# Constants of accumulating DMAs in SBUF instead of DRAM, 26 exponential slots instead of 30, output weights loaded later, two more packs on VectorE

## The chip, the cores and the metric

The kernel runs on one core of a Trainium2 chip. The metric is the device time of one execution in microseconds, as the median of several runs. The profile is one execution of its own, and its span reaches from its first to its last instruction.

## The reference

```
x = A_x                                    # 2048 tokens, 512 features; also the input of branch B
g = sigmoid((x * gate_w).sum(-1))          # one gate for each token
a = softmax(q k^T * 16 ** -0.5) v @ A_wo   # 32 heads of 16, over all 2048 keys; q, k, v from A_wqkv
b = (phi(q) (phi(k)^T v)) / (phi(q) z) @ B_wo   # linear attention, 32 heads of 16
    # phi(q) = [softmax(q w_phi), softmax(-q w_phi)], z = sum over tokens of phi(k)
return g * a + (1 - g) * b
```

Everything is in bf16. The softmax attention of branch A is by far the larger part: 32 x 2048 x 2048 scores.

## The kernel before

The softmax part is cut into 512 packs. A pack is one key tile of 128 tokens, four heads and 512 queries: four score tiles ("units") of 128 x 512. 16 packs in a row (the 16 key tiles) make a group, and 32 groups (4 query chunks x 8 sets of four heads) make the whole. TensorE computes the scores (L1025, `_scores`). They become weights in one of two ways:

- On ScalarE: one activation (L1073, `_exp`) takes two units from PSUM and writes exp(score) into two slots of the ring `ET`, which has `NSLOT` slots of 512. The value product of a pack (`_pv`, L1158) reads four slots and adds to the group's PSUM bank. A slot is free again once the pack that used it has been multiplied, so the exponential of the unit at place x waits for the value product of the unit at place x - NSLOT. TensorE may compute scores two activations ahead: scores k wait for exponential k - 2.
- On VectorE, for the packs that the bits of `AWAY` select in each group (131 of 512): a tensor_scalar from PSUM (L963, `_vector_bits`) writes the bits of a bf16 power of two into `va`, as uint16. Then the sum of four value products with shifted bits approximates the exponential (`_pv_terms`, L1158): `va` itself; two copies `vp` that VectorE makes by adding 62 and 95 to the bits (L980, `_vector_terms`, two packs at a time where there are two), one value side scaled; and `va` once more after 30 (`FIRST_SHIFT`) was added to it in place. This last addition is made by an accumulating DMA from POOL's queue (L1140), 512 KB, that reads a tensor `step` full of the constant 30. Only for the packs from 496 on does VectorE do it (L1146). `va` has room for three pairs of packs.

`step` is a tensor in DRAM: POOL fills a row of `va` with 30 (L593), and SP's queue stores it (L594). The first accumulating DMAs wait for this store.

Branch B (projections, softmax features by `_b_quad`, products, transposing DMAs) and the projections of branch A (L675, L748) run between the attention's instructions on the same engines. ScalarE has 16 long activations of branch B (L1331) among its exponentials. The gate's products stand in L772, and its exponential, L786, is on ScalarE. The output matmuls (L1461 with `WoB`, L1507 with `WoA`) come per query chunk, the first ones after more than half of the groups.

The order of the instructions on every engine is not written down but planned when the program is built (`Plan.order`): a list scheduler with a cost for each operation, a due pack (`prio`), an earliest pack (`rel`), a delay after the end (`lat`), and shifts of single due times by name in the table `SHIFT` ("p37" is the value product of pack 37, "b33" the bits of pack 33, "x33" its late value products, "i33" its first one and its DMA). At run time every engine follows its list in order and waits on semaphores. Accumulating DMAs are planned with a landing time of 6.2 us (`LANDING`), 3.2 us apart (`PACE`), and each waits for the landing of the second to last before it. SP's queue issues all other DMAs: x, weights, the splitting of q into padded tiles (L711), the turning of the normalised attention (L1198, L1413), the transposes of branch B and the output.

Of the kernel before, what the change touches and what calls it, by code (L numbers as in the profile page):

```python
# [404 lines left out]
class _Kernel:  # L405
    RING = 4
    NSLOT = 30
# [42 lines left out]
    def _memory(self, ctx):  # L450
# [55 lines left out]
        self.step = nc.dram_tensor("step", [P, self.NB * QCH], U16, kind="Internal").ap()  # L506
# [23 lines left out]
    def _loads(self):  # L530
# [24 lines left out]
        for j in range(1, self.NQC):  # L555
# [9 lines left out]
                 writes=[self.b_WoA], prio=-1, lat=4.0)  # L565
        self.dma("SP", "wob", lambda e: e.dma_start(self.WoB[:], self.B_wo.rearrange("(q p) j -> p q j", p=P)),
                 writes=[self.b_WoB], prio=-1, lat=4.0)

    def _consts(self):
# [22 lines left out]
        row = self.va[:, self.NVA - 1, 1].rearrange("p n q -> p (n q)")  # L592
        o = op("POOL", lambda e: e.memset(row, FIRST_SHIFT), 2.0, prio=-60)  # L593
        self.o_step = self.dma("SP", "step", lambda e: e.dma_start(self.step, row), cost=0.6, deps=[o], prio=-43, lat=6.0)  # L594
# [164 lines left out]
    def _gate(self):  # L759
# [44 lines left out]
    AWAY = (21, 22, 19, 29, 22, 27, 28, 29, 27, 31, 29, 23, 31, 22, 31, 31, 15, 31, 30, 29, 27, 29, 31, 14, 23, 31, 29, 31, 29, 23, 31, 31)  # L804

    SHIFT = (
# [761 lines left out]
```

## Time and profile before

| | |
|---|---|
| Time, median of 3 runs | 760.13 us (753.11 to 762.33) |
| Profiled execution, its own time | 753.26 us |
| Its span | 751.5 us |
| Granted TensorE clock | 0.997 |
| PE busy | 728.1 us (97%) |
| DVE busy | 700.2 us (93%) |
| ACT busy | 731.8 us (97%) |
| POOL busy | 126.5 us (17%) |
| Moved by DMA | 88.34 MB, of which 66.07 MB in queue q0 (accumulating DMAs) |
| HBM | 70.27 MB read, 2.62 MB written |

PE is TensorE's matmul, PEld its weight load, DVE is VectorE, ACT is ScalarE, POOL is GpSimd and SP is SyncE. A group of the profile's page reads: line, engine, operation, written tile <- read tile, count, then busy time, mean duration of one in ns, and the idle time of the engine just before the group with what ended most of it. Matmuls that use only a part of the array overlap, and so do successive activations, so that the sum of durations can be more than the time that passes. The chain is followed back from the last instruction: at each step to what released it, or to the instruction before it on its engine.

### The profile page before, as it was taken

How to read it: one execution, taken by the hardware profiler on the slowest of the kernel's cores; microseconds unless marked ns; L12 is line 12 of the kernel's file. 1: busy time of each engine (PE TensorE's matmuls, PEld its weight loads, DVE VectorE, ACT ScalarE, POOL GpSimd, SP SyncE). 2: the span in 40 equal slices, each digit the busy share in tenths (PEclk: the TensorE clock that was granted, in tenths of full speed). 3: DMA queues.
4: the chain of work that ended last, by engine and by line, in shares of the span. 5: the costliest groups of instructions: out<-in, count | busy, mean ns of one | idle time of the engine just before them, and what ended most of it. 6: DMA issues, size and time to landing. Idle time of an engine off the chain costs nothing.

```text
span 751.5 us, 16620 instructions
## 1 busy us (share of the span) xinstructions
PE 728.1 (97%) x6969; PEld 225.6 (30%) x6969; DVE 700.2 (93%) x1119; ACT 731.8 (97%) x782; POOL 126.5 (17%) x144
## 2 busy tenths in 40 slices
PE   8999999999999999999999999999999999999998
PEld 3233333333322232232222223233222232222222
DVE  6789999789999999999999999998999989999896
ACT  5899999999999999999999999999999999999996
POOL 4201011201101112021112210121121111121200
PEclk9999999999999999999999999999999999999999
DMA  9754246634655739485597973979496886786950
GB/s 225 200 89 82 31 84 113 104 60 63 118 96 82 144 57 161 85 139 89 96 159 140 177 123 54 181 132 158 70 168 120 140 145 114 143 154 111 170 98 29
DMA packets 108315, 88.34 MB, mean 118 GB/s; under 512 B 84944, under 2 KB 91472, under 8 KB 108240
## 3 DMA queue, kind: packets, MB, share of 16 engines
q0 software_dynamic: 18144, 66.07, 50.8%
q1 hardware_dynamic: 88368, 20.69, 15.2%
q8 instruction: 54, 0.88, 0.5%
q10 hardware_dynamic: 1728, 0.52, 0.3%
q14 instruction: 21, 0.17, 0.1%
HBM read 70.27 MB, written 2.62 MB: 97 GB/s over the span
## 4 chain that ended last, share of the span: by engine, by line
ACT 87%; PE 8%; DMA 4%; DVE 1%; POOL 0%; issue 0%; DVEq 0%; POOLq 0%
ACT ET L1073 83%; ACT bq L1331 4%; PE ps L1025 3%; PE ps L1158 3%; DMA WT<-nb 2%; DMA va<-step 1%; PE ps L675 1%; DMA xT<-in_A_x_dram 1%; PE ps L1461 1%; PE ps L748 0%; PE ps L1507 0%; DVE qT L731 0%; DVE bq L1302 0%; POOL bq L608 0%; ACT xT L1517 0%; DVE nb L1443 0%
## 5 line engine op out<-in xcount | busy, mean ns | idle before, releaser
L1073 ACT ACTIVATE ET<-ps 128x1024 bf16<-128x1024 f32 x762 | 703.9, 1141 | 10.0 <-PE ps L1025 9.7
L1025 PE MATMUL ps<-qT,kT 32*128 32x512 bf16 x2048 | 340.8, 385 | 11.1 <-ACT ET L1073 6.5
L963 DVE TENSOR_SCALAR va<-ps 128x512 uint16<-128x512 f32 x524 | 333.6, 680 | 16.5 <-PE ps L1025 15.3
L1140 POOL DMA_DIRECT2D va<-step x126 | 117.0, 988 | 583.1 <-DVE vp L980 246.5
L1025 PEld LDWEIGHTS ps<-qT,kT 32*128 32x128 bf16 x2048 | 90.1, 91 | 287.6 <-ACT ET L1073 227.3
L980 DVE TENSOR_SCALAR vp<-va 128x4096 uint16<-128x4096 uint16 (+1 forms) x148 | 159.9, 1094 | 5.8 <-PE ps L1158 5.2
L1158 PE MATMUL ps<-ET,V 128*32 128x512 bf16 x1524 | 145.6, 386 | 0.3 <-DVE bq L1302 0.2
L1158 PE MATMUL ps<-va,V 128*32 128x512 bf16 x1048 | 99.1, 386 | 2.4 <-DMA va<-step 2.0
L1158 PE MATMUL ps<-vp,vc 128*32 128x512 bf16 x1048 | 92.3, 387 | 2.6 <-DVE vp L980 2.5
L675 PE MATMUL ps<-WB,xT 128*128 128x512 bf16 x192 | 57.5, 384 | 0.0
L1158 PEld LDWEIGHTS ps<-ET,V 128*32 128x32 bf16 x1524 | 37.7, 94 | 64.5 <-issue 56.9
L1158 PEld LDWEIGHTS ps<-va,V 128*32 128x32 bf16 x1048 | 25.8, 95 | 39.0 <-issue 28.7
L675 PE MATMUL ps<-xT,WA 128*128 128x512 bf16 (+1 forms) x128 | 37.2, 381 | 0.1
L1158 PEld LDWEIGHTS ps<-vp,vc 128*32 128x32 bf16 x1048 | 23.5, 95 | 36.0 <-issue 21.4
L1331 ACT ACTIVATE bq<-bq 128x2048 bf16<-128x2048 bf16 x16 | 32.0, 2009 | 0.0
L1302 DVE CAST bq<-ps 128x512 bf16<-128x512 f32 x32 | 21.8, 682 | 3.8 <-PE ps L675 3.5
L1179 DVE STREAM_TRANSPOSE T<-ps 128x512 f32<-128x512 f32 x32 | 22.7, 709 | 2.6 <-PE ps L1158 2.5
L748 PE MATMUL ps<-WA,xT 128*128 128x128 bf16 x256 | 22.9, 221 | 0.0
L1165 PE MATMUL ps<-kT,zero 128*32 128x512 bf16 x240 | 22.7, 385 | 0.0
L1461 PE MATMUL ps<-WoB,WT 128*128 128x512 bf16 x64 | 19.6, 384 | 0.4 <-issue 0.4
L1329 DVE TENSOR_TENSOR bq<-bq,btree 128x2048 bf16<-128x2048 bf16 x16 | 19.5, 1218 | 0.0
L1507 PE MATMUL ps<-WoA,onTA 128*128 128x512 bf16 x64 | 18.6, 382 | 0.0
(84 smaller groups left out, 302.0 us busy)
## 6 DMA issues: line engine op xcount, KB each, us to landing
va<-step POOLq DMA_DIRECT2D x126, 512.0 KB, 6.0
turned<-T SPq DMA_DIRECT2D x240, 8.0 KB, 3.1
qT<-qs SPq DMA_DIRECT2D x120, 16.0 KB, 3.3
WB<-in_B_wqkv_dram SPq DMA_DIRECT2D x1, 1536.0 KB, 9.4
out_dram<-WB SPq DMA_DIRECT2D x12, 128.0 KB, 4.0
WA<-in_A_wqkv_dram SPq DMA_DIRECT2D x3, 384.0 KB, 5.7
step<-va SPq DMA_DIRECT2D x1, 512.0 KB, 8.5
WoA<-in_A_wo_dram SPq DMA_DIRECT2D x1, 512.0 KB, 10.3
```

The source lines that it names most:

```text
L675: ins = e.matmul(self._bank(job)[:, 0:n], lhs(c), rhs(c), start=(c == 0), stop=(c == 3))
L748: ins = e.matmul(self._bank(job)[:, P * tt:P * tt + P], self.xT[:, c, QCH * j + TOK * tt:QCH * j + TOK * tt + TOK], self.WA[:, 2, c, P * c ...
L963: parts.append(op("DVE", lambda e, j=j, job=job: e.tensor_scalar(self.va[:, pair, side, j, :], self._bank(job), SCALE * LOG2E * 128.0, (12 ...
L980: self.plan.op("DVE", lambda e, k=k, shift=shift: e.tensor_scalar(flat(self.vp[:, k]), flat(self.va[:, pair]), float(shift), None, op0=ALU ...
L1025: return e.matmul(out, self.kT[32 * i:32 * i + 32, cp, kt * TOK:(kt + 1) * TOK], self.qT[32 * i:32 * i + 32, s, :], start=True, stop=True, ...
L1073: o = plan.op("ACT", lambda e: e.activation(self.ET[:, a % NS:a % NS + n, :], self.ps[:, self._ring(a):self._ring(a) + n, :], ACT.Exp, sca ...
L1140: add = self.dma("POOL", f"add{p}", lambda e: e.dma_start(va.rearrange("p n q -> p (n q)"), self.step, accum_op=ALU.add), cost=self.ADD, d ...
L1158: ins = e.matmul(self._bank(ot)[32 * i:32 * i + 32, :], V[:, v0:v0 + 32], tile(), start=(kt == 0), stop=(kt == self.NT - 1), tile_position ...
L1165: ins = e.matmul(self._bank(ot)[32 * i:32 * i + 32, :], self.zero[:], self.kT[:, 0, 0:QCH], start=False, stop=False, tile_position=(0, 32 ...
L1179: op("DVE", lambda e: e.transpose(T1[:, side].rearrange("p b s -> p (b s)"), src()), 0.635, deps=last, writes=[b_T1[side]], name="n_t1", p ...
L1331: op("ACT", lambda e, side=side: e.activation(sides[side], sides[side], ACT.Exp, scale=1.0 - 2 * side), self.c_act(2048) + 0.04, reads=[bu ...
L1461: return e.matmul(self._bank(job), self.onTB[:, pr, tt * TOK:tt * TOK + TOK], self.WoB[:, pr, :], start=(pr == 0), stop=False)
```

## The change

`step` becomes a tensor in SBUF: 4 KB for each of the 128 partitions, filled by POOL, with no store. `NSLOT` goes from 30 to 26, which is 4 x 1 KB for each partition less. The loads of `WoA` and `WoB` get an earliest pack of 50 and 80 and a due pack of 60 and 90. `AWAY` selects 133 packs instead of 131 (one more in groups 6, 8, 21, 23 and 28, one less in groups 4, 14 and 27; in other groups it is only other packs), and `SHIFT` is another table, so that the planned order differs on every engine.

```diff
-    NSLOT = 30
+    NSLOT = 26
...
-        self.step = nc.dram_tensor("step", [P, self.NB * QCH], U16, kind="Internal").ap()
+        self.step = sb("step", [P, self.NB * QCH], U16)
...
         self.dma("SP", "woa", lambda e: e.dma_start(self.WoA[:], self.A_wo.rearrange("(q p) j -> p q j", p=P)),
-                 writes=[self.b_WoA], prio=-1, lat=4.0)
+                 writes=[self.b_WoA], prio=60, rel=50, lat=8.0)
         self.dma("SP", "wob", lambda e: e.dma_start(self.WoB[:], self.B_wo.rearrange("(q p) j -> p q j", p=P)),
-                 writes=[self.b_WoB], prio=-1, lat=4.0)
+                 writes=[self.b_WoB], prio=90, rel=80, lat=8.0)
...
-        row = self.va[:, self.NVA - 1, 1].rearrange("p n q -> p (n q)")
-        o = op("POOL", lambda e: e.memset(row, FIRST_SHIFT), 2.0, prio=-60)
-        self.o_step = self.dma("SP", "step", lambda e: e.dma_start(self.step, row), cost=0.6, deps=[o], prio=-43, lat=6.0)
+        self.o_step = op("POOL", lambda e: e.memset(self.step[:], FIRST_SHIFT), 2.0, prio=-10)
...
-    AWAY = (21, 22, 19, 29, 22, 27, 28, 29, 27, 31, 29, 23, 31, 22, 31, 31, 15, 31, 30, 29, 27, 29, 31, 14, 23, 31, 29, 31, 29, 23, 31, 31)
+    AWAY = (22, 22, 19, 29, 18, 30, 30, 30, 31, 31, 15, 23, 31, 28, 27, 31, 15, 31, 27, 15, 29, 31, 31, 15, 29, 31, 15, 27, 31, 30, 31, 31)
     SHIFT = (
-        ("p30", 2), ("e0", 12), ("p47", -10), ("e3", 4), ("g5", -13.5), ("p251", -1), ("p253", -11.5), ("p274", -4),
...
+        ("p8", 1), ("p13", -5), ("x25", 3), ("p16", -2.5), ("g0", -0.5), ("i5", 13.5), ("p14", 1), ("p20", -6.5),
...
-        self.b_va[self.NVA - 1][1].readers = [self.o_step]
...
-            add = self.dma("POOL", f"add{p}", lambda e: e.dma_start(va.rearrange("p n q -> p (n q)"), self.step, accum_op=ALU.add),
+            add = self.dma("POOL", f"add{p}", lambda e: e.dma_start(va.rearrange("p n q -> p (n q)"), self.step[:], accum_op=ALU.add),
```

221 rows, old and new, of the table SHIFT are left out of this document.

## The prediction

> **What bounds the kernel now.** I first read the busy shares, the queues and the groups of the page, to find the engine without slack.
>
> ```profile
> PE 728.1 (97%) x6969; PEld 225.6 (30%) x6969; DVE 700.2 (93%) x1119; ACT 731.8 (97%) x782; POOL 126.5 (17%) x144
> ...
> q0 software_dynamic: 18144, 66.07, 50.8%
> ...
> ACT 87%; PE 8%; DMA 4%; DVE 1%; POOL 0%; issue 0%; DVEq 0%; POOLq 0%
> ...
> L1073 ACT ACTIVATE ET<-ps 128x1024 bf16<-128x1024 f32 x762 | 703.9, 1141 | 10.0 <-PE ps L1025 9.7
> ...
> L963 DVE TENSOR_SCALAR va<-ps 128x512 uint16<-128x512 f32 x524 | 333.6, 680 | 16.5 <-PE ps L1025 15.3
> L1140 POOL DMA_DIRECT2D va<-step x126 | 117.0, 988 | 583.1 <-DVE vp L980 246.5
> L980 DVE TENSOR_SCALAR vp<-va 128x4096 uint16<-128x4096 uint16 (+1 forms) x148 | 159.9, 1094 | 5.8 <-PE ps L1158 5.2
> ```
>
> ScalarE's exponentials set the time: 762 of them are on 83% of the chain, and ScalarE is idle for only 751.5 - 731.8 = 19.7 us. So a change can save little unless it takes exponentials away; it can lose more easily. ScalarE's waits and the chain in order of time say where the idle time is:
>
> ```profile
> ACT ET L1073 <- PE ps L1025: 9.7, 6, 5.5
> ACT xT L1517 <- PE ps L1507: 4.5, 1, 4.5
> ```
>
> ```profile
> 22.41 8.16 DMA va<-step
> 30.61 0.93 PE ps L1158 x8
> ...
> 34.08 54.22 ACT ET L1073 x59
> ```
>
> 5.5 of the 9.7 us is the start, before the first scores. The chain shows the next largest: the first accumulating transfers, issued at 22.41, take 8.16 us to land while WB, WoA and WoB (2.5 MB) are loading. TensorE stands at L1158 until 30.61, and ScalarE loses 1.96 + 0.92 = 2.9 us by 34.07, as its timeline says. The remaining 9.7 - 5.5 - 2.9 = 1.3 us are three small gaps. The x59 row also gives the price of an exponential in a full stretch: 54.22 / 59 = 0.92 us, less than the 1.14 us of one, since they overlap.
>
> **Part 1: two more packs on VectorE (131 to 133).** A pack is 4 score tiles of 512, two exponentials of 1024. So 4 exponentials go: 4 x 0.92 = 3.7 us off ScalarE. VectorE gets 8 more L963 (8 x 0.68 = 5.4 us) and, as more packs come in pairs, four more L980 of 4096 at 1.22 and four fewer of 2048 at 0.68 (+2.2 us): 7.6 us. Two more transfers are issued, 0.9 us each, on a POOL queue that is 17% busy. Whether VectorE hides its 7.6 us is seen from the stretches:
>
> ```profile
> 200.00:300.00 100.00, 97.92 (x952) 28.29 (x952) 98.60 (x151) 100.00 (x108) 18.23 (x19) 1.00 0.61 104
> 400.00:500.00 100.00, 97.44 (x929) 29.92 (x926) 96.76 (x157) 99.99 (x108) 19.08 (x20) 1.00 0.77 134
> 500.00:520.00 20.00, 19.62 (x212) 6.29 (x208) 18.73 (x33) 20.00 (x23) 5.68 (x6) 1.00 1.00 171
> 580.00:612.00 32.00, 31.06 (x328) 9.71 (x324) 29.54 (x53) 31.38 (x35) 6.40 (x8) 1.00 0.97 157
> ```
>
> Columns are busy time of PE, PEld, DVE, ACT and POOL, then the clock, the share of the DMA engines and GB/s. Per group of 16 packs the count moves by +1 in groups 6, 8, 21, 23 and 28 and by -1 in 4, 14 and 27. Groups 21 and 23 lie near 480 to 560 us, where VectorE is 94 to 97% busy: two packs bring 2 x 3.8 us there, against about 2.7 us of idle time and no relief but what the planner moves elsewhere. That costs between 0 (the work moves) and 5 us (nothing moves). I take 1.5, nearer to hidden, because a pack's tiles are made up to three pairs ahead.
>
> **Part 2: 26 slots instead of 30.** An exponential now waits for the value products of the units 26, not 30, places before it: 13 exponentials (12 us) of reach instead of 15 (13.8). Most exponentials keep a wide margin. But in the changed order on TensorE two have none. Exponential 71 now needs the product of pack 37 (with 30 slots it would be pack 36, which stands far earlier), and TensorE's queue there reads: scores 72, the 16 gate products of L772, pack 37. Scores 72 wait for exponential 70, so nothing of this can run early. Exponential 77 needs pack 40 (with 30 slots pack 39, which is earlier), behind: scores 78, three projection halves of L675, pack 40. The prices are rows of the trace: scores 0.33 (0.39 with the tail of the pipeline), the gate about 1.0, four value products 0.33, L675 1.02 for four, so 0.26 each:
>
> ```profile
> 10.68 1.02 PE ps L675 x4
> ```
>
> ```profile
> 24.88 1.05 PE L772 MATMUL ps<-xT,bq 128*32 128x512 bf16 x16
> ```
>
> With about 0.3 us for the two hand-overs (an estimate, from the 0.04 us between PE and ACT at 34.07 and the gaps of some 0.2 us on the other side), ScalarE stands 0.3 + 0.33 + 1.0 + 0.33 = 2.0 us, and 0.3 + 0.33 + 6 x 0.26 + 0.33 = 2.5 us. Queued behind it on ScalarE are the next exponentials and the gate's own; on them wait TensorE's next scores. None of the long activations of L1331 (1.79 us), which in the old order cover such places, stands near these two. Together +4.5 us, at least 3 (if hand-overs are free and pipelines overlap) and at most 7 (VectorE has 15 evictions and 2 short terms at 0.68, a long term at 1.22 and a value copy at 0.54, 13.3 us, in the 12 exponentials before exponential 71, which last 11.0 us).
>
> **Part 3: weights later, no write of the constants.** The store of the constants (512 KB) and WoA and WoB (1 MB) leave the first 20 us; POOL's fill of the constants (1.80 us) moves behind other fills, ahead of 10 idle us. On SP's queue the loads are moved past the gate's 16 copies and two query splits. In the changed order the first transfer of constants is issued at about 20 us (after the first products of its pack), the second at about 23, and they are used behind scores 22 and 23, at 28 to 30 us. With landing times of 6 to 7 us the 2.9 us gap shrinks to about 0.5: -2.4 (bounds 0 and -2.9). The moved loads now fall between transfers of L1140 at 75 to 120 us; each can hold one back by the 2 us that the early crowding cost (8.16 against 6.0), which the margins of 3 us between issue and use there cover. Uncovered it would be 2 us each; I add nothing.
>
> **Part 4: constants read from SBUF.** This has no row. The landing now:
>
> ```profile
> DMA to landing us min/median/max: 5.3/6.0/11.0
> ```
>
> Queue q0 holds the 16 engines for 50.8% of 751.5 us, 382 us for 126 transfers: 3.03 us each, at 512 KB. A transfer reads the constants, reads the destination and writes it. Lower bound: the pace of the mix at 20 to 30 us, 307 GB/s at full share, gives 1.7 us. Upper bound: today 1.0 of the 1.5 MB is on the SBUF side, 346 GB/s in 3.03 us; if that were that side's limit, 1.5 MB would take 4.55 us. I take 3.03, since the nearest row is the transfer itself: same rows of 4 KB, same engine, same sum. Faster landings gain next to nothing, as TensorE waits for va only 2.0 + 3.0 us in all and its order is fixed; slower ones are the second rival.
>
> **The sum**, against the profiled execution (753.26 us, span 751.5): -3.7 + 1.5 + 4.5 - 2.4 = -0.1, so 753.2. The four executions shown (753.26, 760.13, 753.11, 762.33) have a mean of 757.2, 3.9 above the profiled one; a median may fall in either group, so I add that: **757 us**, against the 760.13 us of before no difference that a measurement of this kernel tells (about 2%, 15 us). Its own range is 748 to 767.
>
> **Rivals.**
>
> *All gaps close.* If the two stops of part 2 don't show, the early gap and the three small ones vanish and VectorE hides everything: 753.3 - 3.7 - 2.9 - 1.3 = 745. For it: these gaps all hang on crowded DMA engines. Against: the order of TensorE makes the stops unavoidable. It lies at the 2% bound from the median of before.
>
> *Constants from SBUF make the transfers slower.* Place: the bursts of L1140, where transfers follow each other at the pace of the engines. 24 of them already wait 49.9 us for a landing, and the engines are 97 to 100% taken at 500 to 520 and 580 to 612. The trace has 15 transfers in 57 us (374 to 431) and bursts of 8 to 9 in 26 to 35 us at 493, 537, 578 and 690. Up to about 3.8 us each they nearly fit; at 4.55 they overrun by 11 + 10 + 6 + 7 + 6 us and some 5 earlier: +45, near 800 us. Half way, at 4.2, about +25: 780. For it: all three streams are then on one side. Against: the read of HBM goes away. The Trainium skill's page "DMA: Bandwidth & Descriptors", section "Where 436 GB/s comes from", speaks against the change: the 16 SBUF ports are the bottleneck, at 435 GB/s. By it a transfer would take an estimated 2.4 us if only its two reads count and 3.6 us if the write counts too, and the time by the sum would be 757 to about 760. No run so far shows it.
>
> *The slots cost more than two stops.* Where VectorE is late, further exponentials wait for their slot; about 8 more stops of 2.2 us would give 775. For it: VectorE's 98.6% at 200 to 300 us. Against: elsewhere the margins in the order are as wide as before.
>
> **Chances.** Forecast 0.55; gaps close 0.12; slower transfers 0.23 (770 to 800); more stops 0.10. Faster by over 2%: 0.12; within: 0.55; slower: 0.33. The range, 744 to 788, reaches down to closed gaps and up past the middle of the slower transfers.
>
> **What would show it.** Right: 758 exponentials at 0.92 us; ScalarE idle for about 2 us twice between 75 and 90 us with TensorE at L772 and L675 ahead of it; no long wait at 28 to 34 us; landing near 6 us and q0 near 51%. Wrong: landing over 7.5 us with q0 above 60%; ScalarE waiting for L1158 in many places; VectorE idle less than 1% from 480 to 560 us.

## The result, and the profile after

The changed kernel takes 779.14 us (median of 4 runs, 777.55 to 781.4), the kernel before beside it 761.23 us (4 runs, 753.11 to 763.21): a ratio of 1.0294, interval 1.024 to 1.0349. It is slower by some 3%, where no change was forecast; the time lies inside the range given, but only because that range reached up to a rival that did not happen: by luck. Ratios here and below compare the fast executions alone, with a 95% interval, so they can differ from the ratio of the two medians. The profiled execution took 777.55 us, its span is 775.8 us, 24.3 us more than before.

The page of the changed kernel, the lines that answer to those shown of before:

```profile
PE 731.5 (94%) x6940; PEld 224.7 (29%) x7008; DVE 707.3 (91%) x1127; ACT 729.8 (94%) x778; POOL 129.8 (17%) x146
...
q0 software_dynamic: 18432, 67.12, 45.5%
...
ACT 60%; PE 22%; DVE 11%; DMA 4%; SPq 2%; issue 1%; DVEq 0%
...
L1071 ACT ACTIVATE ET<-ps 128x1024 bf16<-128x1024 f32 x758 | 702.9, 1138 | 34.8 <-PE ps L1023 30.2
...
L962 DVE TENSOR_SCALAR va<-ps 128x512 uint16<-128x512 f32 x532 | 339.6, 680 | 23.0 <-PE ps L1023 21.4
L1138 POOL DMA_DIRECT2D va<-step x128 | 119.2, 1017 | 607.0 <-DVE vp L979 364.2
```

ScalarE is busy for 2.0 us less and the span is 24.3 us longer, so it now idles 46.0 us instead of 19.7. All of the loss is idle time of ScalarE. TensorE is behind most of it (30.2 us before exponentials), but TensorE itself is idle more too (94% instead of 97%): something holds it. SP's queue (SPq), no part of before's chain, has 2% of this one. ScalarE's waits (us in total, times, longest):

```profile
ACT ET L1071 <- PE ps L1023: 30.2, 24, 6.4
ACT xT L1515 <- PE ps L1505: 5.9, 1, 5.9
ACT ET L1071 <- PE ps L1156: 4.1, 2, 2.3
```

The busy times by stretch tell where (columns as in the prediction: PE, PEld, DVE, ACT, POOL, then clock, DMA share, GB/s). First before, then after:

```profile
0.00:75.00 75.00, 71.23 (x650) 27.45 (x650) 58.06 (x102) 64.17 (x70) 16.66 (x26) 0.98 0.68 149
440.00:500.00 60.00, 58.88 (x521) 18.26 (x513) 57.91 (x94) 59.99 (x65) 7.50 (x9) 1.00 0.72 124
500.00:530.00 30.00, 28.46 (x287) 8.95 (x283) 26.44 (x49) 29.12 (x32) 5.68 (x6) 1.00 0.81 135
600.00:645.00 45.00, 44.37 (x411) 13.35 (x409) 42.83 (x72) 44.38 (x49) 7.84 (x9) 1.00 0.75 124
```

```profile
0.00:75.00 75.00, 71.77 (x679) 28.17 (x687) 60.68 (x98) 66.83 (x72) 18.58 (x27) 1.00 0.59 130
75.00:100.00 25.00, 24.33 (x213) 7.74 (x214) 20.36 (x42) 21.01 (x23) 1.72 (x2) 1.00 0.40 72
400.00:440.00 40.00, 37.37 (x389) 11.20 (x388) 34.44 (x59) 37.42 (x42) 9.31 (x9) 0.96 0.86 141
440.00:500.00 60.00, 55.99 (x445) 15.19 (x448) 52.73 (x83) 53.64 (x57) 6.97 (x8) 0.89 0.59 115
500.00:530.00 30.00, 23.65 (x227) 7.35 (x225) 22.68 (x39) 23.45 (x27) 4.36 (x5) 0.89 0.61 110
600.00:645.00 45.00, 38.09 (x355) 10.43 (x356) 33.79 (x56) 35.66 (x39) 7.80 (x9) 0.85 0.75 126
```

ScalarE's idle time is the stretch less its ACT column. It changes by -2.7 up to 75 us, +4.0 at 75 to 100 (before had 25.00 of 25), +2.6, +6.4, +5.7 and +8.7 in the four stretches between 400 and 645, and +1.4 at the output. That makes 26.1 of the 26.3 us. The first two were forecast, the four in the middle (23.4 us) were not. ScalarE's timeline of the changed kernel (start, time, group, idle before):

```profile
76.46 1.94 ACT L1071 ACTIVATE ET<-ps 128x1024 bf16<-128x1024 f32 x2 [1.82 <-PE ps L1156]
...
84.45 9.27 ACT L1071 ACTIVATE ET<-ps 128x1024 bf16<-128x1024 f32 x10 [2.27 <-PE ps L1156]
...
473.52 1.02 ACT L1071 ACTIVATE ET<-ps 128x1024 bf16<-128x1024 f32 x1 [1.85 <-PE ps L1023]
...
525.95 1.02 ACT L1071 ACTIVATE ET<-ps 128x1024 bf16<-128x1024 f32 x1 [5.60 <-PE ps L1023]
...
632.70 1.02 ACT L1071 ACTIVATE ET<-ps 128x1024 bf16<-128x1024 f32 x1 [6.36 <-PE ps L1023]
634.21 1.02 ACT L1071 ACTIVATE ET<-ps 128x1024 bf16<-128x1024 f32 x1 [0.48 <-PE ps L1023]
635.72 1.02 ACT L1071 ACTIVATE ET<-ps 128x1024 bf16<-128x1024 f32 x1 [0.49 <-PE ps L1023]
```

With one at 428 (1.53) the four late stops are 15.3 us. The other 9.5 us of the 24.8 that ScalarE idles in the four stretches come behind them: after a stop exponentials follow each other at 1.51 us (632.70, 634.21, 635.72) and not at 0.92. The clock column says why. The stretch behind the stop at 473, in the view by stretch:

```profile
473.60:487.20 13.60, 13.13 (x70) 2.42 (x63) 8.48 (x14) 9.13 (x9) 0.68 (x1) 0.50 0.56 115
```

TensorE's granted clock is 0.50 there, though it is busy for 13.13 of 13.60 us. In the whole execution it is at half for 37.5 us behind the four stops, against 3.4 us before (at 31 us; the last microseconds are left aside).

What holds TensorE at 520 us is told by the chain (start, time, what) and by SP's and VectorE's lines of the timeline:

```profile
504.60 0.61 SPq L1196
...
517.69 0.93 SPq L1196
518.67 4.88 DMA WT<-nb
...
524.51 0.63 PE ps L673
```

```profile
503.92 14.70 SPq L1196 DMA_DIRECT2D turned<-T  x16
518.67 4.35 SPq L1411 DMA_TRANSPOSE WT<-nb  x2
...
523.57 0.48 DVE L1441 SCALAR_TENSOR_TENSOR nb<-ps,ghb,rb 128x256 bf16<-128x256 f32 x1 [5.65 <-DMA WT<-nb]
```

SP issues the 16 copies that turn a group's attention (L1196, 8 KB each); they take 14.70 us of its queue. Right behind them stand two transposes of `nb`. `nb` has two buffers, so VectorE cannot write the next one (L1441) before the transpose has landed; it stands for 5.65 us, with it TensorE (a projection at L673 needs the bank that VectorE has not read, 5.55 us), then ScalarE. The stops at 428 and 632 have the same chain. At 473 what is late behind the copies is a query split (L709); there the copies take 12.10 us, no longer than the 12.90 at this place before. VectorE's waits for the transposes of `nb` in all, before and after:

```profile
DVE nb L1443 <- DMA WT<-nb: 3.3, 3, 1.4
```

```profile
DVE nb L1441 <- DMA WT<-nb: 13.4, 3, 5.7
```

In the old order the neighbours on SP's queue at the same place read:

```profile
501.33 12.71 SPq L1198 DMA_DIRECT2D turned<-T  x16
514.09 3.93 SPq L1413 DMA_TRANSPOSE WT<-nb  x2
```

Two things differ: the copies take longer, and the slack behind them (the work that VectorE has left until it needs the transpose) is smaller. In the planned order of the changed kernel VectorE has 31, 28, 36 and 34 instructions between the one that releases the copies of the groups from 257, 321, 385 and 449 and the one that needs the transpose behind them; before it is 51, 35 and 39 for the first three, and nothing waits behind the fourth. At 707.3 / 1127 = 0.63 us each, the 28 of the second group are 17.6 us and the 35 before are 22. The copies and the landing of one transpose (median 4.9 us now, 5.6 before) need 14.7 + 4.9 = 19.6 now and 12.7 + 5.6 = 18.3 before: an estimate, since VectorE waits for other things too. In the traces, from the start of VectorE's instruction that releases the copies (501.10 now, 497.35 before) to the landing of the transpose (523.54 and 520.66), the second group takes 22.4 us now and 23.3 before: its copies also stood some 2 to 3 us behind a query split, and this transpose landed faster now (4.88 us against 6.57). So at this one place the fewer instructions make the difference; what the longer copies add, the experiments tell.

### The profile page after: what moved, and what is told of

It is laid out like the page before. It is cut to its first block, busy times and chain, and to the rows that moved or that the text cites. A ratio compares the mean times of both kernels' runs of the same rounds, so it can differ in the third digit from the quotient of the medians.

```text
span 775.8 us, 16622 instructions
## 1 busy us (share of the span) xinstructions
PE 731.5 (94%) x6940; PEld 224.7 (29%) x7008; DVE 707.3 (91%) x1127; ACT 729.8 (94%) x778; POOL 129.8 (17%) x146
## 3 DMA queue, kind: packets, MB, share of 16 engines
q0 software_dynamic: 18432, 67.12, 45.5%
## 4 chain that ended last, share of the span: by engine, by line
ACT 60%; PE 22%; DVE 11%; DMA 4%; SPq 2%; issue 1%; DVEq 0%
ACT ET L1071 57%; PE ps L1023 9%; PE ps L1156 7%; DVE va L962 5%; ACT bq L1329 3%; DMA WT<-nb 2%; PE ps L673 2%; DVE vp L979 2%; SPq L1196 2%; PE ps L746 1%; DMA qT<-qs 1%; PE ps L1505 1%; DMA xT<-in_A_x_dram 1%; DVE btree L1318 1%; PE ps L1459 1%
## 5 line engine op out<-in xcount | busy, mean ns | idle before, releaser
L1071 ACT ACTIVATE ET<-ps 128x1024 bf16<-128x1024 f32 x758 | 702.9, 1138 | 34.8 <-PE ps L1023 30.2
L1023 PE MATMUL ps<-qT,kT 32*128 32x512 bf16 x2048 | 344.8, 390 | 20.1 <-ACT ET L1071 8.0
L962 DVE TENSOR_SCALAR va<-ps 128x512 uint16<-128x512 f32 x532 | 339.6, 680 | 23.0 <-PE ps L1023 21.4
L1138 POOL DMA_DIRECT2D va<-step x128 | 119.2, 1017 | 607.0 <-DVE vp L979 364.2
L979 DVE TENSOR_SCALAR vp<-va 128x4096 uint16<-128x4096 uint16 (+1 forms) x148 | 162.4, 1108 | 4.5 <-PE ps L1156 4.2
L1156 PE MATMUL ps<-va,V 128*32 128x512 bf16 x1064 | 101.7, 392 | 0.6 <-DMA va<-step 0.3
L1156 PE MATMUL ps<-vp,vc 128*32 128x512 bf16 x1064 | 94.5, 389 | 0.4 <-DVE vp L979 0.4
L673 PE MATMUL ps<-WB,xT 128*128 128x512 bf16 x161 | 51.2, 390 | 10.8 <-DVE nb L1441 5.7
L673 PE MATMUL ps<-xT,WA 128*128 128x512 bf16 (+1 forms) x106 | 31.9, 375 | 3.3 <-issue 2.1
L1441 DVE SCALAR_TENSOR_TENSOR nb<-ps,ghb,rb 128x256 bf16<-128x256 f32 x32 | 14.8, 480 | 13.7 <-DMA WT<-nb 13.4
L673 PEld LDWEIGHTS ps<-WB,xT 128*128 128x128 bf16 x192 | 11.4, 97 | 28.7 <-issue 15.4
```

The lines of the kernel that those rows point to most:

```text
L673: ins = e.matmul(self._bank(job)[:, 0:n], lhs(c), rhs(c), start=(c == 0), stop=(c == 3))
L962: parts.append(op("DVE", lambda e, j=j, job=job: e.tensor_scalar(self.va[:, pair, side, j, :], self._bank(job), SCALE * LOG2E * 128.0, (12 ...
L979: self.plan.op("DVE", lambda e, k=k, shift=shift: e.tensor_scalar(flat(self.vp[:, k]), flat(self.va[:, pair]), float(shift), None, op0=ALU ...
L1023: return e.matmul(out, self.kT[32 * i:32 * i + 32, cp, kt * TOK:(kt + 1) * TOK], self.qT[32 * i:32 * i + 32, s, :], start=True, stop=True, ...
L1071: o = plan.op("ACT", lambda e: e.activation(self.ET[:, a % NS:a % NS + n, :], self.ps[:, self._ring(a):self._ring(a) + n, :], ACT.Exp, sca ...
L1138: add = self.dma("POOL", f"add{p}", lambda e: e.dma_start(va.rearrange("p n q -> p (n q)"), self.step[:], accum_op=ALU.add), cost=self.ADD ...
```

## The experiments

The theory: the order on SP's queue puts copies ahead of urgent transposes, and constants in SBUF make the copies longer. Rivals: the source alone, the 26 slots, or the rest of the order. Ratios are to the kernel before on the same chip, in the same set of runs.

**The copies behind the transposes, in the changed kernel.**

```diff
+        for name in ('dma_on257', 'dma_on321', 'dma_on385', 'dma_on449'):   # SP's queue
+            i = next(k for k, o in enumerate(sp) if o.name == name)
...
+            sp[i:i + 3] = [sp[i + 1], sp[i + 2], sp[i]]     # both nb transposes first
```

> The changed kernel with its own order, but on SP's queue the 16 turning copies of four groups (those of packs 257, 321, 385 and 449) are moved behind the two transposes of nb that followed them. Theory S (the new order puts the transposes of nb behind 16 copies of 0.6 to 1.5 us each, and VectorE needs them too soon; each stop also halves TensorE's clock): the stops near 420 to 433, 471 to 487, 521 to 529 and 627 to 641 us go, 753 to 760 us, ScalarE idle about 22 us. Rival V (VectorE's load or the 26 slots set the time): no change beyond 5 us, 773 to 780. The two stops near 75 to 85 us (1.8 and 2.3 us) stay under both.

Measured: 756.2 us, ratio 0.9982 (0.9945 to 1.0019). The whole loss is gone with four moves in one queue; the constants in SBUF, the 26 slots and the 133 packs are still there. The stretches of its profile (an execution of 763.68 us, the longest of ten):

```profile
440.00:500.00 60.00, 56.61 (x404) 13.51 (x407) 47.78 (x75) 49.39 (x50) 6.97 (x8) 0.80 0.58 105
500.00:530.00 30.00, 29.20 (x301) 9.21 (x301) 29.07 (x51) 30.00 (x34) 5.90 (x7) 1.00 0.73 135
...
600.00:645.00 45.00, 44.37 (x446) 12.82 (x439) 43.30 (x73) 44.89 (x50) 10.41 (x11) 1.00 0.73 135
```

ScalarE has no gap any more at 500 to 530. What remains, though the expectation had it go too, is the stop at 471, behind the query split, and the half clock after it: 10.6 us at 440 to 500 in this execution.

**Constants in DRAM, in the changed kernel**, with 26 and with 30 slots; the order stays.

```diff
-        self.step = sb("step", [P, self.NB * QCH], U16)
+        self.step = nc.dram_tensor("step", [P, self.NB * QCH], U16, kind="Internal").ap()
...
-        self.ET = sb("ET", [P, self.NSLOT, QCH], BF16)
+        self.ET = sb("ET", [P, self.SLOTS, QCH], BF16)     # SLOTS = 26 or 30
```

> The changed kernel with its own order and 26 slots, but the constants are again stored to DRAM early and the accumulating transfers read them there. Theory S (order of SP's queue): 773 to 782 us, the 16 copies still take 13 to 14 us to issue, the stops stay. Rival C (transfers that read SBUF slow SP's small copies and transposes, and so cause the stops): the 16 copies take 12 us as before, the stops shrink, 755 to 766 us.

Measured: 765.98 us, ratio 1.0079 (1.0022 to 1.0136). The rival's side came true (755 to 766 us), not that of the order alone (773 to 782). The ten executions spread from 756.14 to 784.36 us.

> As a_dram26, but with 30 slots for exponentials in the space that the constants leave; the order on every engine is the changed kernel's. The two stops near 76 and 84 us (1.8 and 2.3 us) should go, since exponentials 71 and 77 then wait for products that stand earlier: 4 us below a_dram26. If slots also feed the later stops, more: 10 us or more below it.

Measured: 764.83 us, ratio 1.0101 (1.0026 to 1.0176). The source is most of the loss in this order: without it some 1% is left of 3 to 4. The 16 copies are back at 12.05 and 11.8 us (13.6 in the changed kernel), and VectorE's waits for the transposes of `nb` fall from 13.4 us to 4.4 and 4.0; the stop near 520 stays, at 3.0 and 3.9 us on ScalarE. The 4 us that 30 slots were to save don't show: the two can't be told apart, so the slots have no effect that these runs show, and the profile with 30 tells why (75 to 100 us, to be held against the line of after above):

```profile
75.00:100.00 25.00, 24.76 (x216) 7.79 (x214) 20.27 (x42) 21.07 (x23) 1.73 (x2) 1.00 0.40 73
```

ScalarE is busy for 21.07 us with 30 slots and 21.01 with 26. The two waits for a value product are gone, but 1.25 us (the gate) and 2.15 us (scores) stand in their place: TensorE is busy for over 24 of these 25 us, so it reaches each point at about the same time.

**Constants in SBUF and 26 slots in the old order.** In that order some exponentials would wait without end with 26 slots, so 19 value products stand earlier on TensorE.

```diff
-    ... e.dma_start(va.rearrange("p n q -> p (n q)"), self.step, accum_op=ALU.add)
+    ... e.dma_start(va.rearrange("p n q -> p (n q)"), self.step2[:], accum_op=ALU.add)   # in SBUF
...
+            for d in new:                     # value products that free the slots of scores k
+                i = pe.index(d)
+                if i > at:
+                    pe.insert(at, pe.pop(i))
+                    at += 1
```

> The kernel before with its own order, but the accumulating transfers read the constants from SBUF and there are 26 slots; the value products that an exponential would otherwise wait for without end or too long are moved just ahead of its scores (19 places). The early store of the constants and the early loads stay. Theory S: as before, 753 to 765 us, landing about 5.7 us, q0 near 46%. Rival C: the copies take 13.6 us instead of 12.1 and the stops appear, 770 us or more.

Measured: 762.6 us, ratio 1.0082 (1.0047 to 1.0118). The time is on one theory's side, the copies (13.57 us) on the other's. The control, the same kernel with the constants left in DRAM:

```diff
-    ... self.step2[:], accum_op=ALU.add)
+    ... self.step, accum_op=ALU.add)
```

> The kernel before with its own order and constants in DRAM, but with 26 slots, and the value products moved as in b_sbuf26. It parts the 6 us of b_sbuf26. If the constants in SBUF cost them (longer issue of the copies): 755 to 758 us, copies 12 us for 16, as before. If the slots and the moved products do: 761 to 764 us.

Measured: 757.42 us, ratio 1.0008 (0.9972 to 1.0045). So 26 slots and moved products cost nothing, and the source alone costs 0.7%, some 6 us. That is little, and the two intervals barely stay apart, but the traces show its place. SP's timeline and VectorE's waits, first with constants in SBUF, then in DRAM:

```profile
501.05 15.67 SPq L1220 DMA_DIRECT2D turned<-T  x16
516.77 4.42 SPq L1435 DMA_TRANSPOSE WT<-nb  x2
...
DVE nb L1465 <- DMA WT<-nb: 5.9, 2, 3.0
```

```profile
502.53 12.75 SPq L1213 DMA_DIRECT2D turned<-T  x16
515.33 3.31 SPq L1428 DMA_TRANSPOSE WT<-nb  x2
...
DVE nb L1458 <- DMA WT<-nb: 0.6, 1, 0.6
```

Over 15 groups the 16 copies take 13.57 us with SBUF and 11.9 with DRAM. With SBUF, ScalarE stops behind these transposes for 1.86 us until 523.63 and for 2.21 us until 611.57; with DRAM its one stop of that size there, 1.72 us until 515.32, begins at an accumulating transfer that TensorE waits for. Half clock follows all three. So the old order stands close to the edge as well, and the longer copies push it over.

**The changed kernel again, and one more move.** To see how far its time varies, it ran once more unchanged.

> The changed kernel itself, beside the others on one chip. Theory S+C (the order of SP's queue, made worse by copies that take 13.6 us for 16 in place of 12.0 when the constants are read from SBUF): 772 to 782 us, that is above the same order with constants in DRAM (766 us) by 6 us or more. If the source of the constants does nothing: 766 us, as with DRAM.

Measured: 787.29 us, ratio 1.0394 (1.0338 to 1.0449), above both ranges. Its profile has the same stops at 428, 473 and 526 and the fourth at 643, but TensorE is at half clock for 61.4 us in all instead of 37.5. Then the copies of the group from 289 were put behind the query split too, to remove the last stop at 471:

```diff
+        for name, after in (... the four moves ..., ('dma_on289', 'dma_q10')):
...
+            sp.insert(1 + next(k for k, x in enumerate(sp) if x.name == after), o)
```

> The changed kernel with the turning copies behind the two transposes of nb (as in a_nbfirst) and, once more on SP's queue, the copies of pack 289 behind the split of the tenth query tile, for which TensorE waited at 471 us in a_nbfirst. Theory S: the last of the stops after 400 us goes, 749 to 754 us, and the executions lie closer together than 751 to 764. If that stop came from VectorE's load instead, the split is late in this order too: 755 us or more.

Measured: 767.64 us, ratio 1.0132 (1.0078 to 1.0187), a miss. SP's timeline and VectorE's waits:

```profile
423.34 15.78 SPq L1204 DMA_DIRECT2D turned<-T  x16
444.29 1.21 SPq L1419 DMA_TRANSPOSE onTA<-turned  x1
445.54 2.58 SPq L1419 DMA_TRANSPOSE WT<-nb  x2
...
472.22 15.65 SPq L1204 DMA_DIRECT2D turned<-T  x16
487.91 1.07 SPq L1528 DMA_DIRECT2D out_dram<-WB  x2
```

```profile
DVE WB L1526 <- DMA out_dram<-WB: 6.1, 1, 6.1
```

The copies moved last now delay the output stores instead, whose buffers VectorE waits for (6.1 us). A second stop, 4.0 us until 451, stands where an output product waits for the transposes at 445.54. These come behind the copies at 423.34, one of the four groups moved first; with the four moves alone, and the same order up to there, that place cost 0.65 us in the profiled execution. So the moves shift the wait; they don't do away with it.

**Late weights alone, in the old order.**

```diff
+        for name, after in (('dma_woa', 'dma_q1'), ('dma_wob', 'dma_on33')):   # SP's queue
...
```

> The kernel before with the loads of WoA and WoB moved on SP's queue, behind the first query split and behind the first turning copies; nothing else. The 2.9 us in which ScalarE stands at 28 to 34 us should shrink to 0.5 to 1: 2 to 2.5 us below the kernel before. If the store of the constants or WB alone crowd the first transfers, no change.

Measured: 753.92 us, ratio 0.9966 (0.993 to 1.0002). The two waits of 1.96 and 0.92 us at 31 to 34 are gone; ScalarE's timeline:

```profile
27.56 0.23 ACT L794 ACTIVATE onTA<-onTA 128x32 f32<-128x32 f32 x1
27.68 33.10 ACT L1081 ACTIVATE ET<-ps 128x1024 bf16<-128x1024 f32 x36
```

**Both causes undone in the new order, and the best of both in the old one.** The first is the changed kernel with the four moves, DRAM and 30 slots; the second the kernel before with late weights and the copies of 257, 321 and 385 behind the two transposes.

> The changed kernel with both suspected causes undone: on SP's queue the 16 turning copies of the groups from 257, 321, 385 and 449 stand behind the two nb transposes that follow them, and the constants are read from DRAM, with 30 slots (its other parts stay: planned order, 133 packs, later output weights). If the loss was the place of the copies and their longer issue, which add up: 16 copies 12.0 us instead of 13.6, neither the stops at 421, 521 and 627 us nor the two at 76 and 84, and a time below the kernel before, 748 to 753 on a chip where that takes 756.5. If the reordered queue already did all that there was to do (the same order with constants in SBUF took 756.2): 755 to 757. If the planned order of the changed kernel has a weakness of its own elsewhere: 760 or more.

Measured: 754.92 us, ratio 1.0011 (0.9977 to 1.0044): the reordered queue had already done all that shows, and the two causes don't add up. Its profile keeps ScalarE idle for 3.9 us at 75 to 100 and for 6.5 us, with half clock, at 440 to 500.

> The kernel before with two edits of SP's queue: the loads of WoA and WoB stand behind the copies of the second early query split and of group 33, as in the changed kernel, and the 16 copies of the groups from 257, 321 and 385 stand behind the two nb transposes that follow them. If the places of the copies cost in the old order too (its trace shows 0.9 and 0.6 us of stops there): 2.5 to 3 us from the early gap and 1.5 to 4 from the copies, 749.5 to 752.5 where the kernel before takes 756.5. If only the early gap counts: 753.5. If moved copies delay the output products instead: 755 or more.

Measured: 753.37 us, ratio 0.9978 (0.994 to 1.0016). VectorE's wait for the transposes falls from 3.3 to 0.8 us, but a new stop of 2.9 us on ScalarE ends at 623: an output product waits 2.72 us for the next transposes of `nb`, which now come behind the moved copies. Neither this nor late weights alone can be told from the kernel before; no version tried is surely faster.

| Order of SP's queue | constants in DRAM | constants in SBUF |
|---|---|---|
| before | 1.0 (30 slots), 1.0008 (26) | 1.0082 (26) |
| changed | 1.0079 (26), 1.0101 (30) | 1.0294, 1.0394 (both 26) |
| changed, copies behind transposes | 1.0011 (30) | 0.9982 (26) |

So neither cause stands alone. The source costs nothing that shows where the copies have nothing urgent behind them, some 6 us in the old order, and some 15 to 24 us in the new one (differences of the ratios in its row, from several sets of runs).

## Why the prediction was wrong

*Part 1, packs.* VectorE's work grew by 7.1 us (7.6 forecast). ScalarE has 4 exponentials less, but its time on them fell by 1.0 us, not 3.7: one that stands alone takes 1.02 us instead of 0.92, and behind stops many do. The VectorE term of 1.5 us at 480 to 560 can't be told from the stops there.

*Part 2, slots.* Place and size were right: stops of 1.82 and 2.27 us, 4.1 in all, where 2.0 and 2.5 were forecast. That the slots were the cause was not right, so the size was in part luck. With 30 slots ScalarE idles as long in that stretch. TensorE's own work sets the pace there, a property of the new order; the prediction looked at what an exponential waits for and did not ask what would come next if that wait were gone.

*Part 3, late weights.* Right: -2.4 forecast, -2.7 seen up to 75 us, and the gap closes by this step alone in the old order. The moved loads cost nothing that shows, as assumed: ScalarE is busy for all of the 300 us from 100 to 400, as before.

*Part 4, source of the constants.* The transfers did not slow down: 45.5% of 775.8 us for 128 of them is 2.76 us each (3.03 forecast), and the landing reads

```profile
DMA to landing us min/median/max: 4.4/5.7/9.9
```

So the rival of slower transfers names the right side and nearly the right time (780) for a wrong reason. By the Trainium skill's page "DMA: Bandwidth & Descriptors", section "Where 436 GB/s comes from", the prediction had an estimate of 2.4 to 3.6 us; 2.76 lies in it. That the sum has no term for this part was wrong all the same: the price is on SP's queue, 1.5 us for each group of copies, which no line of the prediction looked at.

*The step that failed* is in part 3: "On SP's queue the loads are moved past the gate's 16 copies and two query splits" is all that the prediction says of that queue. The plan reorders it to the end. Every number was at hand: 12.7 us for 16 copies and 3.93 for two transposes on before's timeline of SP, 3.3 us of VectorE's waits for them, and the number of VectorE's instructions in between, which the planned orders give. 28 x 0.63 = 17.6 us against 18.3 would have shown that the slack was gone. In its place the runs showed four stops of 15.3 us behind SP's copies, three of them at the transposes of `nb`, and 23.4 us of new idle time with what follows them; four moves on that queue bring the ratio from 1.0294 to 0.9982. The rivals had a stalled ScalarE by slots and by bandwidth, but none by a queue that issues in order.

*The amplifier* was left out too. The forecast let a stop cost its own length. Here 15.3 us of stops became 24.8 us of idle time with the half clock behind them.

## What to carry to other kernels

Where a change replans the order, walk through every queue that issues in order, the DMA queues first: for each long run of issues write down what stands right behind it, who needs that and how much work that engine has until then. When a wait looks like the price of an edit, ask what the engine behind it would be doing without it; if it is busy anyway, as TensorE was here at 75 to 100 us, the edit may cost nothing there. Where TensorE is nearly full, look at its granted clock behind each of its stops: one can cost more than its own length.

## What the runs showed of the hardware

*Issuing a copy on SP gets slower when accumulating DMAs read SBUF.* The 240 copies take 166.5 to 173.9 us of SP's queue in the seven profiles with constants in DRAM and 192.5 to 199.5 us in the five with SBUF. An issue during which accumulating packets are under way takes 0.74 to 0.79 us on average with DRAM and 0.94 to 0.97 with SBUF; one with none, 0.61 to 0.65 in both. Yet everything lands sooner: in the changed kernel an accumulating transfer in 5.7 us instead of 6.0, a turning copy in 2.7 instead of 3.1. Why issue and landing go opposite ways no run shows.

*The clock can halve after short stops and stay low under load.* In the changed kernel TensorE stood for 1.69 us from 425.76 and for 2.10 from 470.77. Half clock followed for 3.4 and 13.65 us, in the second case with TensorE busy for 13.13 of 13.60. Not every such stop does it: none followed 1.83 us at 28 us (old order, constants in SBUF) or 1.84 us at 150 us (the run with the fifth move). The Trainium skill's page "TensorE: Matmul & The Clock Gate", section "Part 1: The HAM clock gate (the "warmup" mystery)", has the rate halved after an idle window of about 3.4 us and restored after a busy one of that length. The two levels and the length of the steps agree (3.4, 6.8, 13.65 us); that a whole idle window is needed, or that one busy window is enough, does not: the measurement decides. Spells of up to 30.7 us were seen in the second run of the changed kernel, whose profiled time is 11 us longer. The spread between executions fits this, but no run isolates it.
